# Folding the key-sum and denominator matmuls of a linear-attention block into wider KV and numerator matmuls

## Chip, cores, metric

One core of one Trainium2 chip. The metric is the device time of one execution in microseconds (us); a kernel's figure is the median over its runs. An execution is called slow where the record shows a lower granted TensorE clock and a longer time than in the others, and slow ones are not compared with fast ones.

## The reference, cut

A block of linear attention and a gated feed-forward block read the same layer-normed input `xn` (2048 tokens, width 1024); the second gates the first.

```python
def _A_ref(x, wqkv, wo):            # H = 32 heads, Dh = 32
    q, k, v = ...                   # x @ wqkv, split by heads
    phi = lambda t: jnp.where(t > 0, t + 1, jnp.exp(t)) + 1e-6
    pq, pk = phi(q), phi(k)
    kv  = jnp.einsum("bhsd,bhse->bhde", pk, v)
    z   = jnp.einsum("bhsd->bhd", pk)                 # key sum
    num = jnp.einsum("bhqd,bhde->bhqe", pq, kv)
    den = jnp.einsum("bhqd,bhd->bhq", pq, z)[..., None] + 1e-6
    o   = num / den
    return (... o ...) @ wo
...
xn = _layernorm(x)
s = _A_ref(xn, A_wqkv, A_wo)
g = _silu(_B_ref(xn, B_w_gate, B_w_up, B_w_down))     # F = 3584
return x + s * g
```

## The kernel before

A small scheduler records every operation in program order and inserts semaphores. The program has three stages. In stage A, 16 tiles of 128 tokens are normed, transposed, projected to k and v (four blocks of 512 columns, eight matmuls each), and `KVA` adds `pk^T v` into PSUM. In stage B the queries are projected (`QT`, eight matmuls of 512 columns), and per token tile the numerator `NUM`, the division `OD`, a transpose `TO` and the output projection `SM` follow. Stage C is the feed-forward block, about two thirds of the time.

Four heads of 32 channels share each 128-wide group `j`, so `KV` is used with a block-diagonal mask. The parts that the change touches:

```python
def KVA(t):
    phi_flush(("k", t))                       # second half of phi, on VectorE
    for j in range(NJ):                       # NJ = 8
        matmul(kv_reg(j), pk[:, t % 2, j*P:(j+1)*P], vv[:, t % 2, j*P:(j+1)*P], ...)
    for j in range(NJ):                       # key sum: one column of ones
        matmul(ps[:, 7, j:j+1], pk[:, t % 2, j*P:(j+1)*P], ones[:, 0:1], ...)

denv = ps[:, 0, 0:TPB * H]                    # bank 0, which TO uses too
def DEN(tb):                                  # once per block of 4 token tiles
    phi_flush(("q", tb))
    for tl in range(TPB):
        for j in range(NJ):
            matmul(denv[:, tl, j*HPC:(j+1)*HPC], pqT[..., tl*P:(tl+1)*P], Zc[:, j, 0:HPC])
    act:  den_e = denv + 1e-6                 # DENE
    dve:  rden = reciprocal(den_e)            # RDEN, 128 columns

fill(None, upto_tb=0); fill(2); DEN(0); fill(1)      # fill(n): n query projections
NUM(0); OD(0); fill(1)
for tt in range(NT + 1):
    TO(tt); NUM(tt + 1); OD(tt + 1); fill(1); SM(tt - 1); fill(1)
    if tl == TPB - 2: fill(None, upto_tb=tb + 1); DEN(tb + 1)
...
# start:  NWARM = 8 matmuls on zeros, then
for t in (0, 1):
    NM_upto(t + 1); TP(t); TE(t); warm(WARM_TP[t])   # WARM_TP = (4, 2)
NM_upto(3)                                           # norm; statistics of tiles 2 and 3
# ... then the projections of tiles 0 and 1, block by block
```

(Cuts and shortened arguments; `P` is 128, `HPC` is 4, `TPB` is 4.)

## Time and profile before

| | |
|---|---|
| median (5 runs) | 855.04 us (854.65 to 855.55) |
| span of the profiled run | 853.8 us |
| TensorE (PE) busy | 844.0 us, 99% |
| ScalarE, VectorE busy | 27%, 25% |
| first KV accumulation starts | 24.52 us |
| first gate projection (stage C) starts | 270.28 us |

In the lines below, PE is TensorE's matmuls, PEld its weight loads, DVE VectorE, ACT ScalarE and POOL GpSimd; L521 is line 521 of the kernel, and `[0.56 <-ACT den_e L730]` means that the engine had been idle for 0.56 us until ScalarE wrote `den_e`. Kernel before, the busy line of the page and the first line of the chain of work that ended last:

```profile
PE 844.0 (99%) x4550; PEld 405.7 (48%) x4550; DVE 214.7 (25%) x434; ACT 227.5 (27%) x373; POOL 28.9 (3%) x60
...
PE 98%; ACT 1%; DVE 1%; DMA 0%; issue 0%
```

TensorE is the limit throughout. Anything taken off another engine is worth nothing, unless TensorE waited for it. Those waits are few. Kernel before, waits of PE: the line that waited, for whom, total us, times, longest.

```profile
PE ps L521 <- DVE pk L380: 1.6, 1, 1.6
PE ps L485 <- DVE xn L475: 1.6, 2, 1.3
PE ps L769 <- ACT den_e L730: 1.5, 3, 0.6
PE ps L550 <- DVE wz L556: 1.3, 1, 1.3
PE ps L521 <- ACT vv L400: 0.8, 1, 0.8
```

L521 is the KV accumulation, L485 the first transposes, L769 the transpose `TO`.

**Read the cost of a matmul from start to start.** Kernel before, timeline of PE (start us, listed us, engine, line, operation), around the first KV accumulation and around the second denominator group:

```profile
24.52 0.61 PE L521 MATMUL ps<-vv,pk 128*128 128x128 bf16 x8
24.97 0.34 PE L524 MATMUL ps<-ones,pk 128*128 128x1 bf16 x8
25.17 1.02 PE L368 MATMUL ps<-wkv,xnT 128*128 128x512 bf16 x4
...
182.23 0.95 PE L726 MATMUL ps<-Zc,pqT 128*128 128x4 bf16 x32
183.74 0.62 PE L769 MATMUL ps<-ident,o_sb 128*128 128x128 bf16 x8 [0.56 <-ACT den_e L730]
```

The eight key-sum matmuls occupy 25.17 - 24.97 = 0.20 us, although the page lists 164 ns for each and 5.5 us for all 128. The denominator group takes 0.8 us of matmuls, but the transpose after it starts 1.51 us after the group did: it writes bank 0, which ScalarE must first empty.

Why the third KV accumulation waits 1.6 us for `pk`: kernel before, timeline of all engines.

```profile
33.97 1.28 ACT L466 ACT_TABLE_LOAD   x1
35.03 0.21 DVE L460 BATCH_NORM_AGGREGATE mv<-stats 128x2 f32<-128x12 f32 x1
35.27 0.21 ACT L466 ACTIVATE sd<-mv 128x4 f32<-128x4 f32 x1
35.51 0.18 DVE L469 RECIPROCAL rstd<-sd 128x4 f32<-128x4 f32 x1 [0.28 <-ACT sd L466]
35.73 0.55 DVE L475 TENSOR_SCALAR xn<-xring,mv,rstd 128x1024 bf16<-128x1024 bf16 x1
36.19 0.42 DVE L380 TENSOR_TENSOR pk<-tmp_t,r_t 128x512 bf16<-128x512 bf16 x1
...
36.67 0.62 PE L521 MATMUL ps<-vv,pk 128*128 128x128 bf16 x8 [1.61 <-DVE pk L380]
```

The addition that completes `pk` (L380) had its inputs long before. It stands in VectorE's queue behind the normalization of a later tile (L475), and that waits for statistics, a table load and a square root on ScalarE.

### The profile page before, as it was taken

The numbers are of one execution on the slowest core, as the hardware profiler recorded it, in microseconds if no ns is written. First come the engines' busy times: TensorE is split into PE (matmuls) and PEld (weight loads), VectorE is DVE, ScalarE is ACT, GpSimd is POOL, SyncE is SP. The second block draws the span as 40 slices with busy tenths as digits, with TensorE's granted clock in tenths as the row PEclk, the third lists the DMA queues.
The fourth block names the chain that finished last, engine by engine and source line by source line (L and its number), as shares of the span: only waits on it lengthen the run. The fifth ranks groups of instructions, "written<-read, shape, count | busy, mean of one in ns | idle before, by whom it ended". The sixth has DMA issues, their size and how long they took to land.

```text
span 853.8 us, 10456 instructions
## 1 busy us (share of the span) xinstructions
PE 844.0 (99%) x4550; PEld 405.7 (48%) x4550; DVE 214.7 (25%) x434; ACT 227.5 (27%) x373; POOL 28.9 (3%) x60
## 2 busy tenths in 40 slices
PE   8999999999999999999999999999999999999998
PEld 3455554555554444444444444444444444444446
DVE  5644423533331211111111111121121112121111
ACT  4545544645554111101111110111111101111101
POOL 0100000000011000000000000000000010000000
DMA  9610003920003363541254534216354323363020
GB/s 303 227 38 25 1 1 127 372 72 36 38 38 112 99 197 105 192 135 44 69 157 138 178 119 142 68 41 194 125 171 146 94 74 108 121 196 100 7 68 26
DMA packets 79471, 96.10 MB, mean 113 GB/s; under 512 B 2753, under 2 KB 67521, under 8 KB 79425
## 3 DMA queue, kind: packets, MB, share of 16 engines
q1 hardware_dynamic: 76192, 85.47, 31.5%
q0 software_dynamic: 3232, 9.96, 3.3%
q8 instruction: 36, 0.59, 0.3%
q14 instruction: 11, 0.08, 0.0%
HBM read 87.03 MB, written 8.39 MB: 112 GB/s over the span
## 4 chain that ended last, share of the span: by engine, by line
PE 98%; ACT 1%; DVE 1%; DMA 0%; issue 0%
PE ps L368 94%; PE ps L485 1%; PE ps L769 1%; PE ps L521 1%; PE ps L744 1%; PE ps L524 0%; DMA xring<-in_A_x_dram 0%; DVE xn L475 0%; PE ps L726 0%; DVE stats L453 0%; ACT L466 0%; ACT vv L400 0%; ACT e_t L388 0%; ACT xnT L400 0%; ACT r_t L390 0%
## 5 line engine op out<-in xcount | busy, mean ns | idle before, releaser
L368 PE MATMUL ps<-xnT,wu_r 128*128 128x512 bf16 x896 | 211.7, 379 | 0.0
L368 PE MATMUL ps<-xnT,wg_r 128*128 128x512 bf16 x896 | 211.7, 379 | 0.0
L368 PE MATMUL ps<-wd,hT 128*128 128x512 bf16 (+1 forms) x952 | 194.2, 366 | 0.0
L857 DVE TENSOR_TENSOR hT<-ps,sg 128x512 bf16<-128x512 f32 x112 | 77.5, 692 | 317.0 <-PE ps L368 317.0
L849 ACT ACTIVATE sg<-ps 128x512 bf16<-128x512 f32 x112 | 66.9, 597 | 311.7 <-PE ps L368 311.7
L368 PEld LDWEIGHTS ps<-wd,hT 128*128 128x128 bf16 x952 | 93.1, 98 | 100.6
L368 PEld LDWEIGHTS ps<-xnT,wg_r 128*128 128x128 bf16 x896 | 87.7, 98 | 105.7
L368 PEld LDWEIGHTS ps<-xnT,wu_r 128*128 128x128 bf16 x896 | 87.7, 98 | 105.7
L368 PE MATMUL ps<-wkv,xnT 128*128 128x512 bf16 x512 | 115.3, 379 | 0.0
L368 PEld LDWEIGHTS ps<-wkv,xnT 128*128 128x128 bf16 x512 | 48.2, 97 | 53.7
L880 ACT ACTIVATE sy<-ps 128x512 bf16<-128x512 f32 (+1 forms) x34 | 19.4, 572 | 180.8 <-PE ps L368 180.8
L368 PE MATMUL ps<-xnT,wq 128*128 128x512 bf16 x256 | 58.8, 379 | 0.0
L368 PE MATMUL ps<-wo,oT 128*128 128x512 bf16 x256 | 57.7, 379 | 0.0
L887 DVE TENSOR_TENSOR tmpc<-sr,sy 128x512 bf16<-128x512 bf16 (+1 forms) x34 | 13.9, 410 | 167.3 <-ACT sy L880 167.3
L388 ACT ACTIVATE e_t<-ps 128x512 bf16<-128x512 f32 x64 | 38.2, 597 | 60.6 <-PE ps L368 60.6
L394 DVE TENSOR_SCALAR tmp_t<-e_t 128x512 bf16<-128x512 bf16 x64 | 18.8, 294 | 103.0 <-ACT e_t L388 103.0
L368 PEld LDWEIGHTS ps<-wo,oT 128*128 128x128 bf16 x256 | 24.8, 98 | 28.8
L390 ACT ACTIVATE r_t<-ps 128x512 bf16<-128x512 f32 x64 | 37.9, 592 | 0.0
L368 PEld LDWEIGHTS ps<-xnT,wq 128*128 128x128 bf16 x256 | 24.4, 98 | 27.1
L190 POOL DMA_DIRECT2D out_dram<-outt x24 | 13.0, 542 | 423.0 <-DVE outt L890 423.0
L400 ACT ACTIVATE s_sb<-ps 128x512 bf16<-128x512 f32 x32 | 19.1, 597 | 30.7 <-PE ps L368 30.7
L762 DVE TENSOR_TENSOR o_sb<-ps,rden 128x512 bf16<-128x512 f32 x32 | 20.6, 686 | 9.9 <-PE ps L744 9.9
(47 smaller groups left out, 261.8 us busy)
## 6 DMA issues: line engine op xcount, KB each, us to landing
wg_r<-in_B_w_gate_dram SPq DMA_DIRECT2D x28, 1024.0 KB, 5.4
wu_r<-in_B_w_up_dram SPq DMA_DIRECT2D x28, 1024.0 KB, 7.9
wd<-in_B_w_down_dram SPq DMA_DIRECT2D x7, 1024.0 KB, 13.0
wkv<-in_A_wqkv_dram SPq DMA_DIRECT2D x8, 512.0 KB, 8.2
s_scratch<-s_sb POOLq DMA_DIRECT2D x16, 256.0 KB, 2.3
xr<-in_A_x_dram SPq DMA_DIRECT2D x16, 256.0 KB, 2.9
sr<-s_scratch SPq DMA_DIRECT2D x16, 256.0 KB, 3.5
out_dram<-outt POOLq DMA_DIRECT2D x24, 128.0 KB, 2.6
```

The source lines that it names most:

```text
L190: eng.dma_start(o, i).then_inc(s, 16)
L368: ins = e.matmul(out_ap, l, r, start=(start and i == 0), stop=(stop and i == n - 1))
L388: sch.add("act", "E" + tag, lambda e: e.activation(e_ap, bank_ap, ACT.Exp), reads=[bank_ap], writes=[e_ap])
L390: sch.add("act", "R" + tag, lambda e: e.activation(r_ap, bank_ap, ACT.Relu), reads=[bank_ap], writes=[r_ap])
L394: lambda e: e.tensor_scalar(t_ap, e_ap, 1.0, 1e-6, op0=ALU.min, op1=ALU.add),
L400: return sch.add("act", name, lambda e: e.activation(dst, src, ACT.Identity), reads=[src], writes=[dst])
L485: ins = e.transpose(ps16[:, 0, dc * P:(dc + 1) * P], xn[:, i % 2, dc * P:(dc + 1) * P], ident[:, :])
L762: lambda e, dst=dst, src=src, rd=rd: e.tensor_tensor(dst, src, rd, op=ALU.mult),
L849: sch.add("act", "SG%d.%d" % (tb, f), lambda e, sg_ap=sg_ap, gbank=gbank: e.activation(sg_ap, gbank, ACT.Silu), reads=[gbank], writes=[sg_ap])
L857: lambda e, h_ap=h_ap, ubank=ubank, sg_ap=sg_ap: e.tensor_tensor(h_ap, ubank, sg_ap, op=ALU.mult),
L880: sch.add("act", "SY%d.%d" % (tt, pi), lambda e, sy_ap=sy_ap, ybank=ybank: e.activation(sy_ap, ybank, ACT.Silu), reads=[ybank], writes=[sy ...
L887: lambda e, tc_ap=tc_ap, s_ap=s_ap, sy_ap=sy_ap: e.tensor_tensor(tc_ap, s_ap, sy_ap, op=ALU.mult),
```

## The change

The intent: append a column of ones to `v`, so that one accumulation of 129 columns gives KV and the key sum; append the masked key sum to KV as four more columns, so that one matmul of 132 columns gives numerator and denominator. That removes 256 small matmuls. The change has three more parts: an early flush of phi (the addition that completes `pk` enters VectorE's queue before the value blocks are projected), another start (tile 0's first half projection now runs ahead of tile 1's transpose, after 12 warm-up matmuls instead of 8), and a query ring of two banks instead of three (bank 7 is now needed by `NUM`). The diff, cut:

```diff
+    VW = P + 4; KW = P + 1; NW = P + HPC; KPB = 512 // KW; NPB = 512 // NW    # KPB = NPB = 3
-    NWARM = 8
-    WARM_TP = (4, 2)
+    NWARM = 12
+    WARM_TP = (4, 0)
-        vv = alloc("vv", [P, 2, D], BF16)
+        vv = alloc("vv", [P, 2, NJ, VW], BF16)           # columns P:KW set to 1.0 once
-        def KVP(t, blk, split=False):
+        def KVP(t, blk, split=False, mid=None):
+            if blk >= NDW:
+                phi_flush()                              # ahead of the value blocks
             ...                                          # mid() runs between the halves of a split group
 # KVA
-   matmul(kv_reg(j), pk[...j...], vv[:, t % 2, j * P:(j + 1) * P], ...)
-   matmul(ps[:, 7, j:j + 1], pk[...j...], ones[:, 0:1], ...)
+   matmul(kv_reg(j), pk[...j...], vv[:, t % 2, j, 0:KW], ...)
 # start
-        for t in first:
-            NM_upto(t + 1)
-            TP(t)
-            TE(t)
-            warm(WARM_TP[t] if t < len(WARM_TP) else 0)
-        NM_upto(len(first) + 1)
+        NM_upto(1)
+        TP(0)
+        TE(0)
+        warm(WARM_TP[0] if WARM_TP else 0)
+        NM_upto(min(2, len(first) + 1))
+                    def mid(tn=T[idx + 1], idx=idx):     # inside tile 0's first projection
+                        TP(tn)
+                        TE(tn)
+                        ...
+                            NM_upto(len(first) + 1)
-        qring = Ring([1, 2, 7])
+        qring = Ring([1, 2])
-        def DEN(tb): ...                                 # gone, with DENE and RDEN
+        NUMB = [3, 4, 7]
 # NUM
-   matmul(num_reg(j), pqT[...], KV_bd[:, j, :])
+   matmul(num_reg(j), pqT[...], KVZ[:, j, :])            # [masked KV | masked z], 132 columns
 # OD, per token tile, all on VectorE
+   den_e[...] = den columns of 3 banks + 1e-6            # 3 instructions
+   rden = reciprocal(den_e)                              # 32 columns
    o_sb = num * rden                                     # 3 instructions instead of 2
-        DEN(0)
-        fill(1)
         NUM(0)
         OD(0)
         fill(1)
```

More of the change, by code (lines that the diff above doesn't have):

```diff
@@ L245, in _build @@
     assert NJ * HPC == H
+    VW = P + 4
+    KW = P + 1
+    NW = P + HPC
+    KPB = 512 // KW
+    NPB = 512 // NW
     NXR = min(6, NT)
     LD_Q = "pool"
-    NWARM = 8
-    WARM_TP = (4, 2)
+    NWARM = 12
+    WARM_TP = (4, 0)
     WARM_MID = 0
@@ L338, in _build @@
         wo = alloc("wo", [P, NJ, D], BF16)
-        KV_bd = alloc("KV_bd", [P, NJ, P], BF16)
-        Zc = alloc("Zc", [P, NJ, max(HPC, 16)], BF16)
-        den_e = alloc("den_e", [P, TPB, H], FP32)
-        rden = alloc("rden", [P, 2, TPB, H], FP32)
+        KVZ = alloc("KVZ", [P, NJ, NW], BF16)
+        den_e = alloc("den_e", [P, 2, NJ, HPC], FP32)
+        rden = alloc("rden", [P, 2, NJ, HPC], FP32)
         o_sb = alloc("o_sb", [P, 2, D], BF16)
@@ L404, in emit_consts @@
             sch.add("pool", "ones", lambda e: e.memset(ones[:, :], 1.0), writes=[ones[:, :]])
+            sch.add("pool", "vones", lambda e: e.memset(vv[:, :, :, P:KW], 1.0), writes=[vv[:, :, :, P:KW]])
             sch.add("pool", "ident",
@@ L502, in KVP @@
                 warm(WARM_MID)
+                if mid is not None:
+                    mid()
                 mm_group("KV%d.%db" % (t, blk), bank, pairs[HDC:], start=False, stop=True)
@@ L505, in KVP @@
                 mm_group("KV%d.%d" % (t, blk), bank, pairs)
+                if mid is not None:
+                    mid()
             if blk < NDW:
@@ L509, in KVP @@
                 vb = blk - NDW
-                copy_op(VE_ENGS[vb % len(VE_ENGS)], "VE%d.%d" % (t, vb), vv[:, t % 2, vb * DW:(vb + 1) * DW], bank)
+                jpb = DW // P
+                copy_op(VE_ENGS[vb % len(VE_ENGS)], "VE%d.%d" % (t, vb), vv[:, t % 2, vb * jpb:(vb + 1) * jpb, 0:P],
+                        bank.rearrange("p (j c) -> p j c", c=P))
         def kv_reg(j):
-            return ps[:, 5 + j // 4, (j % 4) * P:(j % 4 + 1) * P]
+            return ps[:, 5 + j // KPB, (j % KPB) * KW:(j % KPB) * KW + KW]
         def KVA(t):
@@ L520, in emit @@
                 for j in range(NJ):
-                    ins = e.matmul(kv_reg(j), pk[:, t % 2, j * P:(j + 1) * P], vv[:, t % 2, j * P:(j + 1) * P],
-                                   start=(t == 0 and j % 4 == 0), stop=(t == NT - 1), skip_group_check=True)
-                for j in range(NJ):
-                    ins = e.matmul(ps[:, 7, j:j + 1], pk[:, t % 2, j * P:(j + 1) * P], ones[:, 0:1],
-                                   start=(t == 0 and j == 0), stop=(t == NT - 1), skip_group_check=True)
+                    ins = e.matmul(kv_reg(j), pk[:, t % 2, j * P:(j + 1) * P], vv[:, t % 2, j, 0:KW],
+                                   start=(t == 0 and j % KPB == 0), stop=(t == NT - 1), skip_group_check=True)
                 return ins
             sch.add("pe", "KVA%d" % t, emit,
-                    reads=[pk[:, t % 2, :], vv[:, t % 2, :], ones[:, 0:1]],
-                    writes=[kv_reg(j) for j in range(NJ)] + [ps[:, 7, 0:NJ]])
+                    reads=[pk[:, t % 2, :], vv[:, t % 2, :, 0:KW]],
+                    writes=[kv_reg(j) for j in range(NJ)])
         def WQ():
@@ L648, in _build, with mid @@
             for idx, (t, blk) in enumerate(items):
-                KVP(t, blk, split=(si == 0 and t == T[0]))
+                mid = None
+                if si == 0 and blk == 0 and idx + 1 < len(T):
+                    def mid(tn=T[idx + 1], idx=idx):
+                        TP(tn)
+                        TE(tn)
+                        warm(WARM_TP[tn] if tn < len(WARM_TP) else 0)
+                        if idx == 0:
+                            NM_upto(len(first) + 1)
+                elif si == 0 and idx == 0:
+                    def mid():
+                        NM_upto(len(first) + 1)
+                KVP(t, blk, split=(si == 0 and t == T[0]), mid=mid)
                 kva_tick()
@@ L691, in _build @@
             WG(k)
-        nbk = (NJ + 3) // 4
+        nbk = (NJ + KPB - 1) // KPB
         for hb in range(nbk):
-            j0 = hb * 4
-            j1 = min(NJ, j0 + 4)
+            j0 = hb * KPB
+            j1 = min(NJ, j0 + KPB)
             nj = j1 - j0
-            dst = KV_bd[:, j0:j1, :]
-            src = ps[:, 5 + hb, 0:nj * P].rearrange("p (j c) -> p j c", c=P)
+            reg = ps[:, 5 + hb, 0:nj * KW].rearrange("p (j c) -> p j c", c=KW)
+            dst = KVZ[:, j0:j1, 0:P]
+            src = reg[:, :, 0:P]
             msk = mask_bd[:, :].unsqueeze(1).to_broadcast([P, nj, P])
@@ L702, in _build @@
                     reads=[src, mask_bd[:, :]], writes=[dst])
-        zsrc = ps[:, 7, 0:NJ].unsqueeze(2).to_broadcast([P, NJ, HPC])
-        zmsk = maskc[:, 0:HPC].unsqueeze(1).to_broadcast([P, NJ, HPC])
-        sch.add("dve", "ZCF", lambda e: e.tensor_tensor(Zc[:, :, 0:HPC], zsrc, zmsk, op=ALU.mult),
-                reads=[ps[:, 7, 0:NJ], maskc[:, 0:HPC]], writes=[Zc[:, :, 0:HPC]])
-        qring = Ring([1, 2, 7])
+            zdst = KVZ[:, j0:j1, P:NW]
+            zsrc = reg[:, :, P:KW].to_broadcast([P, nj, HPC])
+            zmsk = maskc[:, 0:HPC].unsqueeze(1).to_broadcast([P, nj, HPC])
+            sch.add("dve", "ZCF%d" % hb, lambda e, zdst=zdst, zsrc=zsrc, zmsk=zmsk: e.tensor_tensor(zdst, zsrc, zmsk, op=ALU.mult),
+                    reads=[reg[:, :, P:KW], maskc[:, 0:HPC]], writes=[zdst])
+        qring = Ring([1, 2])
         def QT(tb, j):
@@ L715, in QT, with num_reg, NUM @@
             phi(("q", tb), "q%d.%d" % (tb, j), bank, pqT[:, tb % 2, j, :], TBW)
-        denv = ps[:, 0, 0:TPB * H].rearrange("p (t h) -> p t h", h=H)
-        def DEN(tb):
+        NUMB = [3, 4, 7]
+        def num_reg(j):
+            return ps[:, NUMB[j // NPB], (j % NPB) * NW:(j % NPB) * NW + NW]
+        def NUM(tt):
+            tb, tl = divmod(tt, TPB)
             phi_flush(("q", tb))
@@ L723, in emit @@
                 ins = None
-                for tl in range(TPB):
-                    for j in range(NJ):
-                        ins = e.matmul(denv[:, tl, j * HPC:(j + 1) * HPC], pqT[:, tb % 2, j, tl * P:(tl + 1) * P],
-                                       Zc[:, j, 0:HPC], start=True, stop=True)
-                return ins
-            sch.add("pe", "DEN%d" % tb, emit, reads=[pqT[:, tb % 2, :, :], Zc[:, :, 0:HPC]], writes=[ps[:, 0, 0:TPB * H]])
-            sch.add("act", "DENE%d" % tb, lambda e: e.activation(den_e[:, :, :], denv, ACT.Identity, bias=1e-6),
-                    reads=[ps[:, 0, 0:TPB * H]], writes=[den_e[:, :, :]])
@@ L732, in DEN @@
-            sch.add("dve", "RDEN%d" % tb, lambda e: e.reciprocal(rden[:, tb % 2, :, :], den_e[:, :, :]),
-                    reads=[den_e[:, :, :]], writes=[rden[:, tb % 2, :, :]])
-        def num_reg(j):
-            return ps[:, 3 + j // 4, (j % 4) * P:(j % 4 + 1) * P]
-        def NUM(tt):
-            tb, tl = divmod(tt, TPB)
-            def emit(e):
-                ins = None
                 for j in range(NJ):
-                    ins = e.matmul(num_reg(j), pqT[:, tb % 2, j, tl * P:(tl + 1) * P], KV_bd[:, j, :],
+                    ins = e.matmul(num_reg(j), pqT[:, tb % 2, j, tl * P:(tl + 1) * P], KVZ[:, j, :],
@@ L745, in emit @@
                                    start=True, stop=True)
                 return ins
-            sch.add("pe", "NUM%d" % tt, emit, reads=[pqT[:, tb % 2, :, tl * P:(tl + 1) * P], KV_bd[:, :, :]],
+            sch.add("pe", "NUM%d" % tt, emit, reads=[pqT[:, tb % 2, :, tl * P:(tl + 1) * P], KVZ[:, :, :]],
                     writes=[num_reg(j) for j in range(NJ)])
+        nnb = (NJ + NPB - 1) // NPB
         def OD(tt):
-            tb, tl = divmod(tt, TPB)
-            for hb in range(nbk):
-                j0 = hb * 4
-                j1 = min(NJ, j0 + 4)
-                w = (j1 - j0) * P
-                nh = w // Dh
-                h0 = j0 * HPC
-                src = ps[:, 3 + hb, 0:w].rearrange("p (h e) -> p h e", e=Dh)
-                dst = o_sb[:, tt % 2, j0 * P:j0 * P + w].rearrange("p (h e) -> p h e", e=Dh)
-                rd = rden[:, tb % 2, tl, h0:h0 + nh].unsqueeze(2).to_broadcast([P, nh, Dh])
+            sl = tt % 2
+            regs = []
+            for hb in range(nnb):
+                j0 = hb * NPB
+                j1 = min(NJ, j0 + NPB)
+                nj = j1 - j0
+                reg = ps[:, NUMB[hb], 0:nj * NW].rearrange("p (j c) -> p j c", c=NW)
+                regs.append((j0, j1, nj, reg))
+                dsrc = reg[:, :, P:NW]
+                ddst = den_e[:, sl, j0:j1, :]
+                sch.add("dve", "DE%d.%d" % (tt, hb),
+                        lambda e, ddst=ddst, dsrc=dsrc: e.tensor_scalar(ddst, dsrc, 1e-6, None, op0=ALU.add),
+                        reads=[dsrc], writes=[ddst])
+            sch.add("dve", "RD%d" % tt, lambda e: e.reciprocal(rden[:, sl, :, :], den_e[:, sl, :, :]),
+                    reads=[den_e[:, sl, :, :]], writes=[rden[:, sl, :, :]])
+            for hb, (j0, j1, nj, reg) in enumerate(regs):
+                src = reg[:, :, 0:P].rearrange("p j (h e) -> p j h e", e=Dh)
+                dst = o_sb[:, sl, j0 * P:j1 * P].rearrange("p (j h e) -> p j h e", h=HPC, e=Dh)
+                rd = rden[:, sl, j0:j1, :].unsqueeze(3).to_broadcast([P, nj, HPC, Dh])
@@ L761, in OD @@
                 sch.add("dve", "OD%d.%d" % (tt, hb),
                         lambda e, dst=dst, src=src, rd=rd: e.tensor_tensor(dst, src, rd, op=ALU.mult),
-                        reads=[src, rden[:, tb % 2, tl, h0:h0 + nh]], writes=[dst])
+                        reads=[reg[:, :, 0:P], rden[:, sl, j0:j1, :]], writes=[o_sb[:, sl, j0 * P:j1 * P]])
         def TO(tt):
@@ L818, in _build @@
                 fill(None, upto_tb=tb + 1)
-                DEN(tb + 1)
         assert not qt_queue
```

## The prediction

> **What bounds the kernel.** TensorE. Busy table: PE 844.0 of 853.8 us (99%), VectorE 25%, ScalarE 27%, DMA far below. The chain of waits is 98% PE, and PE waits in the waits view sum to 9 us. Only PE time and those waits count.
>
> **What is removed (PE timeline, start to start).**
> - Key-sum matmuls, N=1: the eight start at 24.97 and the next group at 25.17, so 0.20 us per tile, though each is listed at 164 ns. 16 tiles: -3.25 us. This is 25 ns per matmul; the Trainium skill, "TensorE: Matmul & The Clock Gate", "Wait, 56ns, not 53.3ns?", gives the same floor for small N; this trace agrees.
> - Denominator matmuls, N=4, 32 per block of four tiles: 0.82 us for the first. At the next three the transpose also waits for ScalarE to empty bank 0 (1.51, 1.51, 1.32 from DEN start to transpose start). Sum: -5.15 us, 1.5 of it waiting.
> - The 1.6 us wait of the third KV accumulation for pk (36.67 us). VectorE queued half of phi behind the normalization, which waits for a ScalarE table load and square root; the new flush puts it ahead. -1.6 us.
> - Start: tile 0's first half projection now precedes tile 1's transpose. xnT of tile 0 is ready at 8.24 us, real matmuls began at 10.26; but tile 1's eviction (about 10.9) and the second weight block's landing (about 12.7) bind next. Estimate -0.95 us.
>
> **What is added.**
> - Columns 129 and 132 instead of 128: 128 x 0.4 ns + 128 x 1.7 ns, an estimate from 216 ns per 512 columns: +0.25 us.
> - VectorE now makes the reciprocal per tile: three 0.18 us adds (as the 32-column mask multiply), one reciprocal near 0.35 us (the 128-column one took 0.95), three multiplies of about 0.5. About 2.3 us against 1.3 now. In the steady loop 6.9 us of PE work lies between NUM and the transpose, so this is hidden. Not at the first tile: only one 1.73 us projection covers it, and VectorE first finishes a phi step. Estimate: TO(0) waits 1.25 us, 0.2 before: +1.05 us.
> - The query ring drops to two banks: ScalarE releases one 1.3 us after its matmuls end, the other bank is filled in 1.73 us; no wait.
> - Instruction order shows a duplicate of tile 3's statistics at the start, with two extra ScalarE table loads (1.28 us each). They fit inside the 7 us of projections that the four-bank ring covers: no cost, least certain.
>
> **Sum:** -3.25 - 5.15 - 1.6 - 0.95 + 0.25 + 1.05 = -9.65 us. All of it lies on PE, the critical path. Predicted 845.4 us, 80% range 843.4 to 847.4: faster by 1.1%, thus within 2%. Chances: faster by over 2% 0.01, within 2% 0.985, slower 0.005.
>
> **What would show it.** KVA to next projection 0.45 us, not 0.65; no PE group after the query projections before NUM; no wait on den_e; no wait for pk near 34 us; one PE wait of about 1.2 us on o_sb near 155 us; accumulating matmuls of 129 columns still 56 ns apart; real projections starting near 8.5 us with the third weight block's projections about 1 us earlier; final 600 us the same.
>
> **What would make it wrong.** Odd widths (129) or rows of 132 columns slowing the stream or weight load; the extra table loads holding a PSUM bank in the first 25 us; the clock still cold at 8.5 us despite 12 warm-up matmuls; the VectorE chain longer than estimated, so that TO waits in each tile; bank 7's new use delaying NUM.

## The result and the profile after

The changed kernel is correct and takes 845.78 us (median of 7 runs, 845.35 to 846.16) against 855.04 us (13 runs of before, 854.65 to 856.13). The ratio is 0.989, with a 95% interval of 0.988 to 0.990; ratios in this text are the mean time of one kernel's fast runs over that of the other's of the same rounds, so they are not quite the ratios of the quoted medians. The prediction was 845.4 us.

Changed kernel, busy line and chain:

```profile
PE 837.0 (99%) x4296; PEld 399.3 (47%) x4296; DVE 225.7 (27%) x517; ACT 229.2 (27%) x372; POOL 29.2 (3%) x61
...
PE 99%; ACT 0%; DVE 0%; issue 0%
```

PE's busy time fell by 7.0 us and the span by 10.3 us (853.8 to 843.5): the rest are waits that went. VectorE has 11 us more to do, and it cost TensorE one wait of 1.0 us. Changed kernel, waits of PE:

```profile
PE ps L560 <- DVE wz L566: 1.3, 1, 1.3
PE ps L787 <- DVE o_sb L780: 1.0, 1, 1.0
PE ps L534 <- ACT vv L404: 0.7, 1, 0.7
PE ps L372 <- ACT xnT L404: 0.5, 2, 0.3
```

The waits for `pk` and `den_e` are gone, and one on `o_sb` is new (L787 is `TO`). Changed kernel, timeline of PE, the first KV accumulation, the third one, and the first numerator:

```profile
23.00 0.62 PE L534 MATMUL ps<-vv,pk 128*128 128x129 bf16 x8
23.46 1.89 PE L372 MATMUL ps<-wkv,xnT 128*128 128x512 bf16 x8
...
33.00 0.62 PE L534 MATMUL ps<-vv,pk 128*128 128x129 bf16 x8
33.47 1.89 PE L372 MATMUL ps<-wkv,xnT 128*128 128x512 bf16 x8
...
151.00 0.63 PE L751 MATMUL ps<-KVZ,pqT 128*128 128x132 bf16 x8
151.47 1.89 PE L372 MATMUL ps<-xnT,wq 128*128 128x512 bf16 x8
154.31 0.62 PE L787 MATMUL ps<-ident,o_sb 128*128 128x128 bf16 x8 [0.95 <-DVE o_sb L780]
```

The accumulation now takes 0.46 us to the next projection instead of 0.65, and the third one no longer waits. The first transpose starts 2.84 us after the projection ahead of it, whose matmuls need 1.73, so that it loses 1.11 us. In the kernel before it lost 0.20 (162.27 - 160.34 = 1.93); kernel before, timeline of PE:

```profile
160.34 1.89 PE L368 MATMUL ps<-xnT,wq 128*128 128x512 bf16 x8
162.27 0.62 PE L769 MATMUL ps<-ident,o_sb 128*128 128x128 bf16 x8
```

VectorE's chain in the gap of the changed kernel, its timeline of VectorE:

```profile
152.04 0.44 DVE L771 TENSOR_SCALAR den_e<-ps 128x12 f32<-128x12 f32 x3
152.52 0.35 DVE L773 RECIPROCAL rden<-den_e 128x32 f32<-128x32 f32 x1
152.90 1.35 DVE L780 TENSOR_TENSOR o_sb<-ps,rden 128x384 bf16<-128x384 f32 x3
```

That is 2.2 us from 152.04 to 154.25 for one token tile. Only the first tile feels it; later tiles have 3.5 to 6.9 us of TensorE work between `NUM` and `TO`.

**A ledger.** In every trace whose kernel has the same code from the first KV accumulation on, the distance from there to the first gate projection repeats to 0.01 us (236.98 or 236.99 us in six profiles of the changed kernel's middle). Stage C takes 583.54 to 583.56 us in all of them. So the middle can be compared at a precision of 0.01 us by one profile each, and all spread between these profiles lies in the first 25 us. The first gate projection, timelines of PE of the kernel before and of the changed kernel:

```profile
270.28 1.89 PE L368 MATMUL ps<-xnT,wg_r 128*128 128x512 bf16 x8
...
259.99 1.89 PE L372 MATMUL ps<-xnT,wg_r 128*128 128x512 bf16 x8
```

Before: 270.28 - 24.52 = 245.76 us. Changed: 259.99 - 23.00 = 236.99 us. The middle gained **8.77 us**; what the start gained needs many runs.

### The profile page after: what moved, and what is told of

Read it like the earlier page. It is cut to its first block, busy times and chain, and to the rows that moved or that the text cites. A ratio compares the mean times of both kernels' runs of the same rounds, so it can differ in the third digit from the quotient of the medians.

```text
span 843.5 us, 10017 instructions
## 1 busy us (share of the span) xinstructions
PE 837.0 (99%) x4296; PEld 399.3 (47%) x4296; DVE 225.7 (27%) x517; ACT 229.2 (27%) x372; POOL 29.2 (3%) x61
## 4 chain that ended last, share of the span: by engine, by line
PE 99%; ACT 0%; DVE 0%; issue 0%
PE ps L372 95%; PE ps L534 1%; PE ps L787 1%; PE ps L490 1%; PE ps L751 1%; PE ps L560 1%; ACT xnT L404 0%; DVE o_sb L780 0%; ACT e_t L392 0%; ACT vv L404 0%; ACT sy L895 0%; DVE rden L773 0%; DVE den_e L771 0%; DVE tmpc L902 0%; DVE tmp_t L398 0%
## 5 line engine op out<-in xcount | busy, mean ns | idle before, releaser
L458 DVE BATCH_NORM_STATS2 stats<-xring 128x6 f32<-128x512 bf16 x34 | 21.6, 677 | 2.5 <-DMA xring<-in_A_x_dram 2.3
```

The costliest lines, as they stand in the source:

```text
L458: ins = e.bn_stats(stats[:, ss, c, 0:6], xring[:, sl, c * CH:(c + 1) * CH])
```

## The experiments

The theory under test is the prediction's sum: key sums, denominators with their waits, early flush and start each give their term independently. The rivals: listed busy time is what counts; the waits only move; the start gives nothing, or is held back by duplicate work. Parts were first put into the kernel before one at a time.

### Key sum alone

```diff
 # the kernel before, with
+        vv = alloc("vv", [P, 2, NJ, VW], BF16)
+   matmul(kv_reg(j), pk[...], vv[:, t % 2, j, 0:KW], ...)     # and no matmuls with ones
+   Zc[:, j0:j1, 0:HPC] = reg[:, :, P:KW] * mask               # DEN stays as it was
```

> The kernel before with the key-sum folded into the KV accumulation and nothing else. My theory (a matmul costs the distance to the next start, 25 ns here): 16 x 0.20 us saved, less 0.05 for the 129th column: 3.2 us faster than before, 851.8 us; the 1.6 us wait for pk near 36 us stays. Rival (a matmul costs its listed busy time, 164 ns a piece overlapping to 5.5 us busy in the group): 5.5 us faster, 849.5 us. Second rival (129 columns or rows of 132 slow the stream): under 2 us faster, with the KV group spaced well over 0.46 us.

Measured: 852.12 us against 855.02 for before in the same rounds, ratio 0.9965 (0.9952 to 0.9977). The middle took 242.78 us, so **-2.98 us**. That is 16 tiles at 0.19 us (0.65 to 0.46). The rival that counts listed busy time (5.5 us) falls, and so does the second, under 2 us. The wait of 1.6 us for `pk` stayed, as expected. Of the 3.25 us, 0.27 came back through the 129th column, more than the 0.05 of the prediction; see the wide accumulation below.

### Denominator alone

```diff
 # the kernel before, with KVZ, NUM, OD and the two-bank query ring of the changed kernel
-        DEN(0)
-        fill(1)
+        # DEN, DENE, RDEN gone; key sums still by matmuls with ones
```

> The kernel before with the denominator folded into the numerator matmuls and nothing else. My theory: 5.15 us of denominator matmuls and bank-0 waits go, 0.2 us come for 132 columns and about 0.8 us for the first transpose (the wait of 0.95 us on o_sb less 0.2 of before): 4.1 us faster, 850.9 us. Rival (only the 128 matmuls of 25 ns count, the waits reappear elsewhere because VectorE has more to do per tile): 2.0 to 2.3 us faster, with waits on o_sb in several tiles.

Measured: 851.74 us against 855.02, ratio 0.9957 (0.9944 to 0.9971). The middle took 241.81 us, so **-3.95 us**; the prediction's terms for this part are -5.15 + 0.2 + 1.05 = -3.9. There was one wait on `o_sb`, of 0.95 us, and none in later tiles, so the rival falls. By the medians its five timed runs gained only 3.3 us. The profiled one started late (first KV accumulation at 24.66 us), and what is left of the other four runs after the middle and stage C says the same of them; such starts are the subject of the start's experiments. Why all five fell on the late side isn't shown.

### Denominators in their own bank

This takes the wait away and leaves the matmuls.

```diff
-        denv = ps[:, 0, 0:TPB * H]...
+        denv = ps[:, 7, 0:TPB * H]...
-        qring = Ring([1, 2, 7])
+        qring = Ring([1, 2])
```

> The kernel before with the denominators in PSUM bank 7 instead of bank 0, which the transposes share (the query ring keeps two banks for it, as in the changed kernel); nothing is folded. My theory: the three waits of the transposes on den_e (0.56, 0.56, 0.37 us) go and nothing comes: 1.5 us faster than before, 853.5 us; the 32 matmuls keep their 0.8 us per block; two query banks cause no wait. Rival (two banks are too few): waits of the query projections on ScalarE, same or slower.

Measured: 853.16 us against 855.50, ratio 0.9975 (0.9961 to 0.9989). The middle took 243.81 us, so **-1.95 us**, where 1.5 was expected. Kernel with the denominators in bank 7, timeline of PE around the second denominator group:

```profile
182.22 0.95 PE L726 MATMUL ps<-Zc,pqT 128*128 128x4 bf16 x32
183.03 0.61 PE L769 MATMUL ps<-ident,o_sb 128*128 128x128 bf16 x8
```

The transpose follows after 0.81 us instead of 1.51. So the wait cost 0.70 us, not the 0.56 that the view lists. The reason is in the view: idle time is counted from the listed end of the last matmul, and a listed end lies about 0.14 us after the moment at which the next matmul could have started (164 ns listed, 25 ns apart). Of the 5.15 us that the denominators cost, 1.95 was thus a bank shared with the transposes, which a change of bank alone would have removed. No wait of the query projections appeared with two banks.

### Early flush alone

```diff
         def KVP(t, blk, split=False):
+            if blk >= NDW:
+                phi_flush()
```

> The kernel before with the early flush of phi ahead of the value blocks and nothing else. My theory: the wait of the third KV accumulation for pk (1.6 us in the waits view, 1.75 from start to start) goes entirely: 1.7 us faster, 853.3 us. Rival (the wait moves to the next transpose or projection, which hangs on the same statistics and table loads): under 0.5 us faster, and a new PE wait on xnT or on a PSUM bank between 33 and 42 us.

Measured: 853.14 us against 855.02, ratio 0.9976 (0.9964 to 0.9989). The middle took 243.90 us, so **-1.86 us**: 1.6 in the view of before, 0.16 more for the listed end as above, and 0.1 from the last accumulation's wait for `vv` (0.8 before, 0.7 here). The wait didn't move; the rival falls.

The three parts sum to -2.98 - 3.95 - 1.86 = -8.79 us, and the whole middle gained 8.77. The parts add up, and nothing in the middle is left unexplained.

### The start alone

> The kernel before with the changed start and nothing else (12 warm-up matmuls, tile 1's transpose inside tile 0's first projection, and with it the duplicate statistics of tile 3). The profile of the changed kernel reached the third weight block 1.5 us sooner, the prediction said 0.95. My theory: a part of the 1.5 is the clock rising at a different moment of the warm-up in the profiled run, so the timed gain is 0.5 to 1.0 us: 854.2 us. Rival (the order alone gives it): 1.5 us faster, 853.5 us in every run. If the duplicate table loads cost anything here: no gain or slower.

The edit is the start part of the diff above in the kernel before. Measured: 854.78 us against 855.02, ratio 0.9991 (0.9978 to 1.0003), in means 854.55 against 855.30. The middle took 245.76 us, as before. The rival, 1.5 us in every run, falls. But the gain is not told from none by itself, so the changed kernel's start was taken apart.

### The changed kernel again

> The changed kernel again, unedited, as the base for the three that follow and as a second sample of its start. Expected 845.8 us within 0.5. If the 1.5 us by which its first profile reached the third weight block sooner was partly a lucky start (clock, landing of the weight blocks), this profile shows another value between 16.1 and 17 us; if it is the order alone, 16.1 again.

Measured: 845.94 us (845.35 to 846.25), and the third weight block was reached at 16.61 us, against 16.09 in the first profile. Its first KV accumulation began at 23.52 us, against 23.00 in the first profile, with the same code. This run's profile shows what the other had not: one projection waited 0.25 us for a weight block to land. A single profile is no measure of the start.

### Without the duplicate statistics

The new order computes tile 3's statistics twice, which costs ScalarE two more table loads. Changed kernel, timeline of ScalarE in the start:

```profile
16.35 1.28 ACT L471 ACT_TABLE_LOAD   x1
17.64 0.21 ACT L471 ACTIVATE sd<-mv 128x2 f32<-128x2 f32 x1
17.87 1.28 ACT L392 ACT_TABLE_LOAD   x1
```

```diff
-            new = list(range(max(k0, st_done[0]), st_target))
+            st_from = max(k0, st_done[0], batch_end(len(first)) if si == 0 else 0)
+            new = list(range(st_from, st_target))
```

> The changed kernel without the duplicate statistics of tile 3 and so without the two extra ScalarE table loads (2.8 us of ScalarE near 16 us). My theory (they fit inside the projections that the four PSUM banks cover): the same time within 0.3 us. Rival (they hold the start back and are why the start gained little): 0.5 to 2.5 us faster.

Measured: 845.86 us against 845.94 for the changed kernel in the same rounds. No difference: the 2.8 us of ScalarE work is covered by projections that four PSUM banks let run ahead, as predicted.

### Fewer warm-ups, the old order, and both

The start has two ingredients, 12 warm-up matmuls instead of 8 and the new order. All four combinations were timed with the changed kernel's middle.

> The changed kernel with 8 warm-up matmuls as before instead of 12. If the 12 matter because the clock is up by the first transpose: transposes of tile 0 at 1.03 us instead of 0.62 in some runs, the first projections at the slow spacing (430 ns), 0.4 to 1.5 us slower. If only the order matters and the start is bound by the landing of the weight blocks: the same within 0.3 us.

> The changed kernel with the start of the kernel before (8 warm-up matmuls, both first transposes ahead of the projections, no duplicate statistics). Timed parts so far sum to 8.3 us of the 9.3 to 9.5 measured for the whole, and the start alone gave only 0.24; the profiles of eight kernels put the third weight block's first matmul at 17.1 to 17.8 us with the old start (mean 17.4 of four) and at 16.1 to 16.9 with the new one (mean 16.4 of five). My theory (the start is worth the predicted 0.95 us on average, spread by the moment at which the clock rises): about 846.8 us, 0.9 slower than the changed kernel. Rival (the start is worth 0.2 to 0.5 as timed alone, and the rest lies elsewhere): 846.1 to 846.4 us.

> The changed kernel with the start order of the kernel before but 12 warm-up matmuls, the missing corner beside the changed kernel (new order, 12), the one with new order and 8, and the one with old order and 8. If the extra warm-ups alone give the start's gain: 845.8 us, as the changed kernel. If both are needed, as I think: the early slow state of the old order (first KV accumulation at 24.5 instead of 24.0 us) no longer occurs, which is worth 0.3 us on average, and the order is worth the rest: 846.0 to 846.3 us, with the first projection at 9.7 us and the first KV accumulation at 24.0.

Since the middle and stage C repeat in every profile, a run's time less their sum is taken as the start of that run with a constant offset. Mean of that remainder in us, over the runs of all kernels with the combination; single runs scatter by 0.38 us (standard deviation):

| | old order | new order |
|---|---|---|
| 8 warm-ups | 25.95 (69 runs) | 25.95 (4 runs) |
| 12 warm-ups | 26.04 (4 runs) | **25.34** (24 runs) |

The medians of the three edited kernels were 846.74 us (new order, 8), 846.15 (old order, 8) and 846.58 (old order, 12), against 845.94 and 845.78 for the changed kernel. Taken alone, the old start with the changed middle lost only 0.2 to 0.4 us, nearer to the rival's 0.2 to 0.5 than to the expected 0.9; the start in the kernel before gained 0.75 in means and 0.24 in medians. The old order with 12 warm-ups missed its expectation, for the late start did occur: the warm-ups then end only with the first transpose's start at 6.35 us, and the first KV accumulation began at 24.50 us. Only the combination shows a gain, about **0.6 us** (0.09 standard error, worked out from the spread of the 69 and the 24 runs). These runs come from several chips; compared within the same rounds alone, the combination's gain over the old start is 0.6 to 0.8 us. The cells with four runs have a standard error of about 0.2 us, so that they are equal to the old start is a weaker statement than the gain of the fourth.

What the profiles show: kernel with the new order and 8 warm-ups, then the changed kernel, timeline of PE in the start.

```profile
1.26 3.59 PE L560 MATMUL ps<-wz 128*128 128x512 bf16 x8 [1.26 <-DVE wz L566]
6.27 1.04 PE L490 MATMUL ps<-ident,xn 128*128 128x128 bf16 x8 [1.42 <-DVE xn L480]
7.10 1.91 PE L560 MATMUL ps<-wz 128*128 128x512 bf16 x4
8.81 1.57 PE L372 MATMUL ps<-wkv,xnT 128*128 128x512 bf16 x4
```

```profile
1.26 4.88 PE L560 MATMUL ps<-wz 128*128 128x512 bf16 x12 [1.26 <-DVE wz L566]
6.11 0.62 PE L490 MATMUL ps<-ident,xn 128*128 128x128 bf16 x8
6.57 1.03 PE L560 MATMUL ps<-wz 128*128 128x512 bf16 x4
7.85 1.04 PE L372 MATMUL ps<-wkv,xnT 128*128 128x512 bf16 x4 [0.25 <-ACT xnT L404]
```

In the first, TensorE still ran slowly at 8.81 us: four warm-ups take 1.91 us instead of 1.03, and the first real projections 1.57 instead of 1.04. In the second it was at full speed by 6.11 us. The Trainium skill, "TensorE: Matmul & The Clock Gate", "What's actually happening", says that the array's clock opens only after a window of sustained activity, that this window runs free of the kernel's start, and that the same kernel therefore shows different numbers of slow matmuls from run to run. These traces agree: the 12 warm-ups of the changed kernel took 4.88 us in its first profile and 4.53 in its second. The old start fell into two kinds: with the unchanged old order and 8 warm-ups, the first KV accumulation began at 23.97 us in three profiles and at 24.51 to 24.66 in the other three. With 12 warm-ups and the new order it lay between 23.00 and 23.77 in six profiles.

It is tempting to blame the pause ahead of the first transpose, which more warm-ups fill. The profiles don't bear that out. Kernel with the early flush alone (8 warm-ups), then the one with the old order and 12, timelines of PE:

```profile
6.21 0.62 PE L485 MATMUL ps<-ident,xn 128*128 128x128 bf16 x8 [1.36 <-DVE xn L475]
...
6.35 1.02 PE L490 MATMUL ps<-ident,xn 128*128 128x128 bf16 x8
```

The first paused and ran at full speed; the second hardly paused and ran slowly. Over all profiles the first transpose was slow in four of seven with 8 warm-ups and in one of seven with 12, which is too few to show that the 12 make it fast. What sets it in a given run stays open.

### A wider accumulation

> One look: the changed kernel with the KV accumulation 168 columns wide (40 columns of ones) instead of 129. In the traces, 128 columns are spaced 55.9 ns, 129 are 57.7 and 132 are 58.4. If the extra over 0.42 ns per column is a fixed cost of leaving the 128-column shape: 168 columns at 55.9 + 40 x 0.42 + about 1.3 = 74 ns. If an odd or unaligned width costs by the column: well over 76 ns. About 1.9 us slower than the changed kernel.

```diff
-    VW = P + 4;  KW = P + 1
+    VW = P + 40; KW = P + 40        # KV accumulation 168 columns wide, 40 of them ones
```

One look, 847.3 us (a single run, state unknown). Mean distance of matmuls in the groups of eight, from their single starts in the traces, the distance from the last to what follows it included: 55.8 ns at 128 columns, 57.9 at 129, 58.7 at 132, 72.6 at 168. From 128 to 168 that is 0.42 ns per column, which is what 216 ns for 512 gives. So there is no fixed cost of leaving 128 columns, and that theory falls. The other, that an odd or unaligned width costs by the column, was hardly tested: 168 columns cost nothing extra, but 168 is neither odd nor badly aligned. The shapes 129 and 132 cost 1.7 and 1.2 ns more than the line, by alternating (129: 55.8, 59.3, 55.8, 59.4 ns within a group). Where the alternation comes from is open, but the code gives a candidate. At 129 and 132 columns the rows of `vv` and `KVZ` lie 132 values of 2 bytes, thus 264 bytes, apart, so that every second `j` starts off a multiple of 16 bytes, and it is the matmuls of odd `j` that take longer. At 128 and 168 columns the rows are 256 and 336 bytes apart, all on multiples of 16, and nothing alternates. No run tested it; rows padded to 136 values would. In sum the folded columns cost 128 x 2.1 + 128 x 2.9 = 0.64 us, not the 0.25 of the prediction.

### A version that beats both

```diff
+        fill(1, upto_tb=0)              # first query projection ahead of the last KV accumulation
         while kva_pending:
             KVA(kva_pending.pop(0)[0])
 ...
         NUM(0)
         OD(0)
-        fill(1)
+        fill(2)                         # two query projections cover VectorE's first chain
```

It also leaves out the duplicate statistics.

> A candidate that beats both: the changed kernel with one more query projection between NUM(0) and TO(0), the last KV accumulation moved behind the first query projection, and no duplicate statistics. My theory: the wait on o_sb (0.95 us) and that of the last accumulation on vv (0.73 us) both go, nothing else moves: 1.6 to 1.7 us faster than the changed kernel, 844.1 us. Rival (waits move on, since the query projections run out one step earlier and VectorE needs 2.6 us per tile against 3.5 us of cover there): under 0.8 us, with new waits on o_sb after 228 us.

Measured: 844.25 us against 845.94 for the changed kernel and 855.46 for before in the same rounds; ratio to before 0.9868 (0.9853 to 0.9882). The middle took 234.99 us, **2.00 us** less than the changed kernel's (1.64 by the idle times that the timeline lists, 0.95 and 0.69, and about 0.15 for each of the two listed ends), against 1.6 to 1.7 expected; by the medians it is 1.7, as this kernel's four runs happened to start later. This kernel's waits of PE, from its profile:

```profile
PE ps L560 <- DVE wz L566: 1.3, 1, 1.3
PE ps L490 <- DVE xn L480: 0.9, 1, 0.9
PE ps L372 <- ACT xnT L404: 0.5, 2, 0.3
```

All three lie in the first 11 us. From there to the end no wait of PE is listed, and no wait appeared where the query projections run out earlier.

## Why the prediction was right

| term | predicted | measured | by |
|---|---|---|---|
| key sums, with the 129th column | -3.25 + 0.05 | -2.98 | key sum alone |
| denominators, 132 columns, first `TO` | -5.15 + 0.2 + 1.05 | -3.95 | denominator alone |
| early flush | -1.6 | -1.86 | early flush alone |
| start | -0.95 | about -0.6 | 24 runs against 69 |
| two query banks | 0 | 0 | denominators in their own bank |
| duplicate statistics | 0 | 0 | without them |
| sum | -9.65 | -9.4 | whole: -9.3 by the medians, -9.4 by the means |

- *TensorE bounds the kernel, and what leaves TensorE is gained in full*: right, and to 0.02 us in the middle, where the parts add up. One number under this heading was wrong: the listed waits sum to 6.8 us, not 9. No term rested on it.
- *Costs from start to start*: right. With listed durations the key sums would have been worth 5.5 us. The skill's page named above gives a floor of about 25 ns for small matmuls ("Wait, 56ns, not 53.3ns?"); the traces show 25 ns for 1 and 4 columns (means of 25.3 to 25.6).
- *Denominators*: right in size. The distance from group to transpose was used, not the listed wait, and so the shared bank was counted whole (1.95 us, called 1.5 in the text).
- *The first `TO` waits on VectorE*: right in place, a little smaller. It lost 1.11 us against 0.2 before (0.91, not 1.05). The chain took 2.2 us, with 2.3 estimated.
- *Early flush*: right in mechanism. The size was low because this term did take the listed wait.
- *Start*: the mechanism was half told, and the gain was about 0.6 us on average rather than 0.95. By the table the order gained only together with the 12 warm-ups; that it needs TensorE already at full speed fits the profiles, but isn't shown. Of the two limits that the prediction named next, tile 1's eviction (ScalarE's copy of its transpose out of PSUM) did bind (0.25 us at 10.46 us in the changed kernel), and a weight block's landing in two of the six profiles (0.25 and 0.42 us). The first profile pair suggested 1.5 us, by luck of the two runs.
- *129 columns 56 ns apart*: wrong, 57.9. The term was +0.25 and measured +0.64.
- The errors of the table's rows (+0.22, -0.05, -0.26, +0.35 us) sum to 0.26 us: they partly cancelled, and to that extent the close total was luck.

## What to carry to other kernels

Cost a small matmul by the distance to the next start; a wait read from idle time is short by the difference between listed duration and spacing. Fold small matmuls into wider ones where TensorE is the limit, but look first for the waits beside them: here a shared PSUM bank cost 1.95 us and an in-order queue on VectorE 1.86, against 2.98 for folding 128 key-sum matmuls. When a change bundles parts, split the trace at fixed points: here the middle repeats to 0.01 us while the start varies by more than half a microsecond, and two single profiles would have put 1.5 us on a part worth 0.6.

## What the Trainium skill lacked or had wrong

- "TensorE: Matmul & The Clock Gate", "Back-to-back issue gap": its formula N / 2.4 + 2.5 ns fits here at 128 columns (55.8 measured, 55.8 computed), at 168 (72.6 and 72.5) and at 512 (216), but not at 129 (57.9 measured, 56.3 computed) and 132 (58.7 and 57.5), where consecutive matmuls alternate between a shorter and a longer distance. The sustained figures that it gives for real streams with weight loads, about 81 ns at 128 columns and 131 at 512, differ from both: the streams here, one weight load per matmul, ran at 55.8 and 216 ns.
- "Perfetto Trace Analysis", "Identifying the Most-Contended Engine", says that matmul occupancy is not a good measure of how close a kernel is to its limit, because matmuls are pipelined. No section of that page says that idle time counted from a listed end understates a wait: 0.56 us was listed where 0.70 was lost.
- No page gives the time of VectorE's reciprocal by the column: 953 ns for 128 fp32 columns and 354 for 32, so 6.2 ns per column, against about 1.1 ns per column for the multiplication from PSUM (553 ns for 384 columns, 415 for 256).
